# Retention by feature in column tiles, and expert blocks of up to 768 slots whose widths are chosen by branches

## The chip, the cores and the metric

The kernel runs on one core of one Trainium2 chip. Times are microseconds (us) of device time. The core has a matrix engine (TensorE, "PE" in the profile; its weight loads are shown apart as "PEld"), a vector engine (DVE), an activation engine (ACT), GpSimd (POOL) and a sync engine (SP), and 16 DMA engines that move data for all of them. A "record" is one matmul as the profile lists it; each float32 product appears as two (the 8 score products of a chunk as 16). In a PE line, 128*64 is the piece of the array in use, rows by columns, and a column tile is a half of its 128 columns used on its own.

## The reference

```python
# 8 batches, 8 heads, 576 positions, head_dim 64; all float32
scores = q @ k.T / 8
ret = scores * gamma[h] ** (i - j)          # for j <= i, else 0
x = (ret @ v)                               # by token: 4608 tokens x 512
logits = x @ w_gate;  local = sigmoid(x @ w_local)
for each batch, for each position s in order:
    e = argmax(logits[s]) if s == 0 or local[s] < 0.5 else the expert of s-1
    out[s] = softmax(logits[s])[e] * (relu(x[s] @ w1[e]) @ w2[e])   # 512 -> 1024 -> 512, 8 experts
```

On these inputs each expert receives 517 to 652 tokens; the prediction lists all eight counts.

## The kernel before

It has three stages. **Retention** runs over 36 chunks of 128 tokens, with a state per head carried from chunk to chunk. Per chunk it transposes k on PE, makes the scores, the outputs by token, and the new state; then it transposes x on PE and makes the logits from it:

```python
for c in range(HP): nc.tensor.transpose(kps[:, c, :], kn[:, c * P:(c + 1) * P], ident)
...
for h in range(H):          # outputs by token: the scores are stationary, 64 columns of V stream
    nc.tensor.matmul(ops[:, h, :], lhsT=sT[:, h % 2, h // 2, :], rhs=vs[:, h * DH:(h + 1) * DH], ...)
...
for c in range(HP):         # state: k of two heads is stationary (only the diagonal blocks are used)
    nc.tensor.matmul(kv[:, c, :], lhsT=kn[r, c * P:(c + 1) * P], rhs=vs[r, c * P:(c + 1) * P], ...)
...
for c in range(DK): nc.tensor.transpose(xps[:, c, :], x[:, c * P:(c + 1) * P], ident)
for c in range(DK): nc.tensor.matmul(lps[:, i, :], lhsT=xT[:, c, :], rhs=wg[:, c, :], ...)
```

**Routing** finds each token's expert and its slot, and the token of each slot, by a long chain of small operations. **Experts**: the slots of an expert are padded to blocks of 256; there are always 25 blocks, the most that any routing can need. Each block loads its expert's weights, gathers its tokens with indirect DMAs, transposes them and runs both layers:

```python
for j in range(NBLK):                               # 25
    e = nc.values_load(eid[0:1, j:j + 1], engines=[ET.SP], ...)   # only the weight loads depend on it
    ... load w1[e], w2[e] (4.2 MB) ...
    for u in range(SUB): ... gather, 4 transposes, copy ...       # SUB = 2
    for m in range(0, FK, 2): ... hidden layer, 256 columns, relu on ACT ...
    for u in range(SUB):
        ... second product (8 matmuls of 512 columns), scale, scatter ...
```

The language's scheduler lays out the order of instructions on each engine; it may place independent work of a later block ahead.

## Time and profile before

| | us |
|---|---|
| time, median of 4 runs | 1039.3 (1037.8 to 1045.9) |
| retention ends at | 250.3 |
| routing, to the first hidden pass | 44.9 |
| experts | 731.2 |
| tail, after the last product | 11.2 |

These are the busy shares of the page of the kernel before, and two of its rows of 40 equal slices of the span (a digit is tenths busy; PEclk is the clock that PE was granted, in tenths of full speed). PE is the bound nearly everywhere, and the dip in the tenth to twelfth slice is routing.

```profile
PE 974.9 (94%) x4918; PEld 719.0 (69%) x4918; DVE 166.8 (16%) x282; ACT 123.8 (12%) x238; POOL 140.7 (14%) x158
...
PE   7999999996479999999999999999999999999995
...
PEclk9999999998589999999999999999999999999998
```

A busy PE says that it executes something, not that it does so at its best rate. So the useful numbers are starts in the timeline, from one group of records to the next, as the prediction uses them.

### The profile page before, as it was taken

The page shows a single profiled execution, that of the slowest core. Times are in us where ns is not written, and L with a number is a line of the kernel's source. Part 1 is how long each engine was busy: PE and PEld are TensorE (multiplying, and loading weights), DVE is VectorE, ACT ScalarE, POOL GpSimd, SP SyncE. Part 2 cuts the span into 40 slices and gives each one's busy share as a digit, 9 for nine tenths or more (in the row PEclk, how much of TensorE's full clock was granted, in tenths as well). Part 3 has the DMA queues.
Part 4 walks back from the last instruction along what each step waited for, and adds up shares of the span by engine and source line. Part 5 has one row for each costly group of instructions (what it writes and reads, how often), then busy time and mean ns, then how long its engine had stood idle before and what let it go on. Part 6 is the DMA issues. An engine that isn't in the chain of part 4 may idle for free. (4 is left out here: it accounts for less than half of the span.)

```text
span 1037.5 us, 12062 instructions
## 1 busy us (share of the span) xinstructions
PE 974.9 (94%) x4918; PEld 719.0 (69%) x4918; DVE 166.8 (16%) x282; ACT 123.8 (12%) x238; POOL 140.7 (14%) x158
## 2 busy tenths in 40 slices
PE   7999999996479999999999999999999999999995
PEld 6999999995466666666666666666666666666662
DVE  2333332324711111010111111010111110010100
ACT  2222222221000000000000000000000000000000
POOL 2111111110021111011111110011111110110000
PEclk9999999998589999999999999999999999999998
DMA  5444444430735544555455544555455544555300
GB/s 201 154 158 157 151 163 162 163 133 32 273 122 203 201 156 148 185 197 177 153 179 187 193 156 153 181 193 188 138 187 203 164 158 160 195 183 167 127 2 0
DMA packets 47509, 166.03 MB, mean 160 GB/s; under 512 B 7006, under 2 KB 7134, under 8 KB 47456
## 3 DMA queue, kind: packets, MB, share of 16 engines
q1 hardware_dynamic: 39168, 142.62, 40.5%
q0 software_dynamic: 8000, 22.56, 6.3%
q8 instruction: 39, 0.64, 0.2%
q14 instruction: 14, 0.11, 0.0%
q10 hardware_dynamic: 288, 0.09, 0.0%
HBM read 146.37 MB, written 22.54 MB: 163 GB/s over the span
## 5 line engine op out<-in xcount | busy, mean ns | idle before, releaser
L395 PE MATMUL hps<-xTs,w1s 128*128 128x256 f32 x1600 | 353.2, 382 | 14.1 <-DVE xTs L389 14.1
L402 PE MATMUL yps<-w2s,hT 128*128 128x512 f32 x800 | 347.4, 592 | 0.0
L395 PEld LDWEIGHTS hps<-xTs,w1s 128*128 128x128 f32 x1600 | 303.0, 191 | 60.2 <-DVE xTs L389 19.8
L402 PEld LDWEIGHTS yps<-w2s,hT 128*128 128x128 f32 x800 | 152.0, 190 | 180.7 <-issue 179.4
L405 DVE TENSOR_SCALAR y<-yps,pslot 128x512 f32<-128x512 f32 x50 | 37.5, 751 | 665.4 <-PE yps L402 665.4
L397 ACT ACTIVATE hT<-hps 128x512 f32<-128x512 f32 x100 | 59.7, 597 | 700.2 <-PE hps L395 700.2
L406 POOL DMA_INDIRECT out_dram<-y,sidx x50 | 50.7, 1014 | 512.0 <-DVE y L405 505.3
L139 PE MATMUL ops<-vs,sT 128*128 128x64 f32 x576 | 82.3, 277 | 0.0
L139 PEld LDWEIGHTS ops<-vs,sT 128*128 128x128 f32 x576 | 72.4, 191 | 4.9 <-issue 0.6
L127 DVE TENSOR_TENSOR sT<-sps,mask 128x512 f32<-128x512 f32 x72 | 46.4, 686 | 159.9 <-PE sps L123 159.9
L383 POOL DMA_INDIRECT xg<-xd,gidx x50 | 48.7, 975 | 164.0 <-PE xgps L388 121.2
L116 POOL TENSOR_TENSOR vs<-ld,dec 128x512 f32<-128x512 f32 x36 | 37.5, 1042 | 190.0 <-PE kv L155 173.2
L123 PE MATMUL sps<-ld,kT 64*128 64x128 f32 x576 | 43.2, 288 | 0.2 <-DVE sT L127 0.2
L161 ACT COPY state<-kv 64x256 f32<-64x256 f32 x64 | 23.4, 366 | 160.2 <-PE kv L155 159.4
L176 PE MATMUL lps<-wg,xT 128*128 128x9 f32 x288 | 38.0, 259 | 1.5 <-ACT xT L174 1.1
L176 PEld LDWEIGHTS lps<-wg,xT 128*128 128x128 f32 x288 | 34.9, 191 | 5.2 <-ACT xT L174 4.7
L123 PEld LDWEIGHTS sps<-ld,kT 64*128 64x128 f32 x576 | 36.3, 190 | 2.9 <-DVE sT L127 0.4
L388 PEld LDWEIGHTS xgps<-ident,xg 128*128 128x128 f32 x200 | 24.2, 146 | 20.1 <-issue 19.5
L155 PE MATMUL kv<-vs,ld 128*128 128x128 f32 (+1 forms) x256 | 35.5, 281 | 0.5 <-ACT state L161 0.5
L146 PE MATMUL ops<-state,ld 128*128 128x128 f32 (+1 forms) x256 | 35.4, 281 | 0.0
L388 PE MATMUL xgps<-ident,xg 128*128 128x128 f32 x200 | 27.7, 282 | 6.6 <-DMA xg<-xd,gidx 6.6
L389 DVE COPY xTs<-xgps 128x512 f32<-128x512 f32 x50 | 32.2, 682 | 7.1 <-PE xgps L388 7.1
(112 smaller groups left out, 271.2 us busy)
## 6 DMA issues: line engine op xcount, KB each, us to landing
w1s<-in_w_dram SPq DMA_DIRECT2D x100, 512.0 KB, 5.5
w2s<-in_w_dram SPq DMA_DIRECT2D x100, 512.0 KB, 8.1
ld<-in_qkv_dram SPq DMA_DIRECT2D x36, 768.0 KB, 4.5
xd<-x SPq DMA_DIRECT2D x36, 256.0 KB, 2.2
xg<-xd,gidx POOLq DMA_INDIRECT x50, 7.3
out_dram<-y,sidx POOLq DMA_INDIRECT x50, 7.5
dec<-in_decay_dram ACTq DMA_DIRECT2D x1, 72.0 KB, 4.6
wg<-in_wgl_dram ACTq DMA_DIRECT2D x1, 18.0 KB, 6.2
```

The source lines that it names most:

```text
L116: nc.gpsimd.tensor_tensor(vs.rearrange("p (h d) -> p h d", h=H), vn.rearrange("p (h d) -> p h d", h=H), dec[:, 1, m, :].unsqueeze(2).to_br ...
L123: nc.tensor.matmul(sps[u][:, c, :], lhsT=kT[r, c, :], rhs=qT[r, c, :], start=True, stop=True, skip_group_check=True)
L127: nc.vector.tensor_tensor(sT[:, u], sps[u], (mask2 if m == MID else mask).unsqueeze(1).to_broadcast([P, HP, P]), op=Alu.mult)
L139: nc.tensor.matmul(ops[:, h, :], lhsT=sT[:, h % 2, h // 2, :], rhs=vs[:, h * DH:(h + 1) * DH], start=(h == 0), stop=(m == 0), skip_group_c ...
L176: nc.tensor.matmul(lps[:, i, :], lhsT=xT[:, c, :], rhs=wg[:, c, :], start=(c == 0), stop=(c == DK - 1), skip_group_check=True)
L383: nc.gpsimd.indirect_dma_start(out=xg, out_offset=None, in_=xd, in_offset=bass.IndirectOffsetOnAxis(ap=gidx[:, s:s + 1], axis=0))
L388: nc.tensor.transpose(xps[:, c, :], xg[:, c * P:(c + 1) * P], ident)
L395: nc.tensor.matmul(hps[:, v, :], lhsT=w1s[:, m + v, c, :], rhs=xT[:, c, :], start=(c == 0), stop=(c == DK - 1), skip_group_check=True)
L397: nc.scalar.activation(hT[:, m:m + 2, :], hps, Act.Relu)
L402: nc.tensor.matmul(yps, lhsT=hT[:, m, u * P:(u + 1) * P], rhs=w2s[:, m, :], start=(m == 0), stop=(m == FK - 1))
L405: nc.vector.tensor_scalar(y, yps, pslot[:, s:s + 1], None, Alu.mult)
L406: nc.gpsimd.indirect_dma_start(out=out, out_offset=bass.IndirectOffsetOnAxis(ap=sidx[:, s:s + 1], axis=0), in_=y, in_offset=None, bounds_c ...
```

## The change

In retention it wants fewer and cheaper PE records: k is also loaded transposed; outputs are made by feature (V stationary with 64 columns, two heads in two column tiles of the array), kv likewise; x by token and the logits come from one product with the identity and the gates side by side. In the experts it wants less padding: one block holds up to 768 slots of an expert, and branches on the number of tokens held choose the width of two hidden passes and how many product groups run.

```diff
-T = 256  # tokens of one expert that go through its weights together
+T = 768
+PASS = T // 2
 NBLK = (NTOK - E) // T + E
+ALWAYS = -(-NTOK // T)
+WIDTHS = (128, 192, 224, 256, 288, 320, 352, PASS)
... (retention)
-            for c in range(HP):
-                nc.tensor.transpose(kps[:, c, :], kn[:, c * P:(c + 1) * P], ident)
+            kT = ld[:, 1].rearrange("p (c s) -> p c s", c=HP)
...
+                for c in range(HP):
+                    for u in range(2):
+                        h = 2 * c + u
+                        nc.tensor.matmul(kv[half(u), c, :], lhsT=kn[r, h * DH:(h + 1) * DH],
+                                         rhs=vs[r, h * DH:(h + 1) * DH], ...)
...
+            for c in range(HP):
+                for u in range(2):
+                    h = 2 * c + u
+                    nc.tensor.matmul(ops[half(u), c, :], lhsT=vs[:, h * DH:(h + 1) * DH],
+                                     rhs=sT[:, u, c, :], ...)
...
+            for c in range(DK):
+                nc.tensor.matmul(nps[:, c, 0:P + E + 1], lhsT=xT[:, c, :], rhs=gates[:, c, :], ...)
... (experts)
+    def by_width(held, base, widths, body):
+        if len(widths) == 1:
+            body(widths[0])
+            return
+        h = len(widths) // 2
+        with tc.If(held > base + widths[h - 1]) as wider:
+            by_width(held, base, widths[h:], body)
+        with wider.Else():
+            by_width(held, base, widths[:h], body)
...
+        by_width(held, 0, WIDTHS, lambda n: hidden(w1s, xT, hT, 0, n))
+        with tc.If(held > PASS):
+            by_width(held, PASS, WIDTHS, lambda n: hidden(w1s, xT, hT, PASS, n))
         for u in range(SUB):
...
+            if u == 0:
+                product()
+            else:
+                with tc.If(held > u * P):
+                    product()
+    for j in range(ALWAYS):          # 6
+        block(j)
+    total = nc.values_load(plan[0:1, 2 * NBLK:], ...)
+    with ExitStack() as rest:
+        for j in range(ALWAYS, NBLK):        # 6 to 12, each inside the branch of the one before
+            rest.enter_context(tc.If(total > j))
+            block(j)
```

## The prediction

> **What bounds the kernel now.** I first read the share of the span by engine: TensorE (PE) 94% busy, no other engine above 16%. Its instructions in order of time show three stages, so I asked for the busy time of each engine in each (columns: stretch; its length; busy us and count of PE, PE weight load, DVE, ACT, POOL; granted clock; DMA share; GB/s).
>
> ```profile
> 5.34:250.30 244.96, 241.58 (x2240) 227.90 (x2240) 71.01 (x108) 62.38 (x136) 37.83 (x38) 1.00 0.45 151
> 250.30:295.17 44.87, 16.23 (x91) 14.27 (x91) 28.52 (x74) 0.44 (x1) 8.24 (x18) 0.58 0.58 212
> 295.17:1027.00 731.83, 717.08 (x2589) 476.79 (x2588) 66.19 (x98) 59.70 (x100) 92.62 (x94) 1.00 0.48 162
> 1027.00:1037.50 10.50, 0.00 (x0) 0.00 (x0) 0.13 (x1) 0.00 (x0) 0.98 (x1) 0.72 0.00 0
> ```
>
> Retention (245 us) and the experts (732 us) are PE-bound, at 98.6% and 98.0% busy. Routing (45 us) is a serial chain, mostly on DVE, at a clock of 0.58. The chain of waits that ended last covers only the final 30 us here, so I price PE work from starts in the timeline: from the start of one group to that of the next, in one retention chunk (start, duration, instruction, count):
>
> ```profile
> 228.26 0.60 PE L172 MATMUL xps<-ident,x 128*128 128x128 f32 x4
> 228.70 0.60 PE L112 MATMUL kps<-ident,ld 128*128 128x128 f32 x4
> 229.13 0.78 PE L139 MATMUL ops<-vs,sT 128*128 128x64 f32 x6
> 229.93 1.06 PE L176 MATMUL lps<-wg,xT 128*128 128x9 f32 x8
> 230.85 0.86 PE L139 MATMUL ops<-vs,sT 128*128 128x64 f32 x6
> 231.64 1.16 PE L123 MATMUL sps<-ld,kT 64*128 64x128 f32 x16
> 232.73 0.66 PE L139 MATMUL ops<-vs,sT 128*128 128x64 f32 x4
> 233.23 1.11 PE L146 MATMUL ops<-state,ld 128*128 128x128 f32 x8
> 234.17 1.06 PE L155 MATMUL kv<-vs,ld 128*128 128x128 f32 x8
> 235.07 0.60 PE L172 MATMUL xps<-ident,x 128*128 128x128 f32 x4
> ```
>
> The period is 235.07 - 228.26 = 6.81 us (36 of them: 245). Each f32 product is two records (8 heads give 16). Per chunk: x transposes 0.44, k transposes 0.43, outputs 0.80+0.79+0.50 = 2.09 (131 ns a record although only 64 columns stream), logits 0.92 (115 ns for 9 columns), scores 1.09 (68 ns), state product 0.94, kv 0.90. Records of 9, 64 and 128 columns cost about the same: with 128 weight columns the weight load paces them. Only the scores, which use 64 rows each, go twice as fast.
>
> One expert block of 256 slots, read in the same way:
>
> ```profile
> 353.27 1.04 PE L388 MATMUL xgps<-ident,xg 128*128 128x128 f32 x8
> 354.88 14.08 PE L395 MATMUL hps<-xTs,w1s 128*128 128x256 f32 x64 [0.57 <-DVE xTs L389]
> 368.80 13.90 PE L402 MATMUL yps<-w2s,hT 128*128 128x512 f32 x32
> 382.53 1.04 PE L388 MATMUL xgps<-ident,xg 128*128 128x128 f32 x8
> ```
>
> Hidden layer: 13.92 us / (64 x 256) = 0.850 ns a column. Second product: 13.73 us for two groups of 128 slots, 6.87 us each. Transposes: 0.52 us a group. Period 29.26; 25 of them are 732. Cost follows slots, padding included: 6400 slots are computed for 4608 tokens.
>
> [...]
>
> **The change, part by part.**
>
> Retention. k arrives transposed too, so 0.43 goes. Outputs are made by feature: 64 columns of V stationary, 128 columns of scores streaming, two heads in two column tiles. Taking the scores' 68 ns for them: 16 x 68 = 1.09 instead of 2.09. kv becomes 16 records with 64 weight columns instead of 8 with 128: at 62 ns (half of a 128-column load plus little) 1.00 instead of 0.90. x and logits: 8 records of 137 columns, 137 x 0.85 = 117 to 120 ns, 0.96, instead of 0.44 + 0.92. Scores 1.09 and state 0.94 stay. Two more mode changes per chunk: 0.15 (a guess: the scores' 68 ns, with their two changes in it, are near the 54 ns that half of 128 columns would take). Sum 5.23 us. DVE (2.06 plus a small reduction), ACT (1.8 less one 0.59 copy) and POOL (1.04) stay below that. DMA moves 1.31 MB per chunk, at 5.2 us 250 GB/s; before, 159 GB/s used half of the engines, and the first 10 us show 314, so 80%: close but hidden. 36 x 5.23 = 188. The start is later: the first load grows from 0.79 to 1.05 MB and shares the engines with a new 1.3 MB decay table (first product at 7.5 instead of 5.3), and two memsets of 6144 elements on POOL (0.8 ns an element from the 288-element one at 0.33 us: 5 us each) may hold back V's scaling. I take 5 us for filling. Retention ends at 201 instead of 250.
>
> Routing. 78 slot groups instead of 50, so the three column operations grow from 2.03 to about 3.17 us (+3.4). The block plan adds some eight small operations at 0.16 to 0.35 us and removes four at 0.17: +1.3. Slot products at half clock, 156 columns instead of 100: +1.5. The first block gathers six groups instead of two, and POOL issues one per 1.25 us: +5. So 45 becomes 56.
>
> Experts. Running the reference's routing on its inputs gives 652, 576, 581, 554, 591, 517, 606 and 531 tokens. All fit one block of 768: eight blocks. Every first pass is 384 wide; the second is 288 once, 224 three times, 192 four times: 4800 columns. Product groups: 6 + 7 x 5 = 41. Transposes: 8 x 6 = 48 groups, unconditional.
> - Hidden: 4800 x 64 x 0.850 ns = 261 (before 25 x 13.92 = 348).
> - Second product: 41 x 6.87 = 282 (before 343).
> - Transposes: 48 x 0.52 = 25 (before 26).
> Sum 568, against 717 of work before. Weights fall from 25 x 4.2 MB to 8 x 4.2 MB; DMA was half idle already, so this buys nothing.
>
> Costs of control flow, which the profile of before can't price:
> - At each block PE waits for ACT's last hidden group (one 0.6 us evacuation plus the hand-over) and DVE's last copy (0.57 above): 1.3. Branches: some 10 compares, and two or three jumps over 500 to 900 PE instructions[...]. [...] 8 x 3.5 = 28.
> - Blocks 6 and 7 stand inside branches, so I expect their gathers can't be placed ahead of the branch: on POOL they follow block 5's last scatter, which waits for the product. Then PE stands still for DVE's 0.75, the scatter's 1.0, a register load, six gathers at 1.25, about 2.4 to land, a transpose and a copy: some 15 us, less 3 of work counted above, plus 1 for the lower clock: 2 x 13 = 26. For blocks 0 to 5 I expect the 12 gather buffers, two blocks' worth, to keep this hidden.
>
> Tail 11.5 (10.5 plus a jump over five blocks). Sum: 201 + 56 + 568 + 28 + 26 + 11.5 = 890 us.
>
> **Rivals.** (a) Column tiles don't overlap: outputs stay at about 115 ns a record, the chunk at 6.0 us, +27: 917. For it: the trace shows only row tiles. [...] (b) Branches dominate: [...]: 990. Against it: PE's queue runs ahead through three PSUM buffers, 7 us of work in a 384-wide pass. (c) Gathers aren't placed ahead in any block: five more stalls of 13 us, 955. In its favour, POOL now waits most of its time for DVE's y in program order; the profile of before shows a scatter, then gathers, interleaved by hand of the scheduler. (d) DMA bounds retention: 1.31 MB at 314 GB/s is 4.2 us, below 5.2, so only the start suffers. (e) Branches nearly free and blocks 6 and 7 prefetched: 890 - 22 - 26 = 842.
>
> **Range and chances.** PE work removed is well measured: about 56 us in retention and 149 in the experts. Some 90 us are given back, two thirds of it estimated. Low end: (e), 842. High end: (c) or half of (b), 965. To lose all 149 us of gain needs more than 18 us per block beyond what I count; I give slower 2% and within 2% 2%.
>
> **What would show it.** A chunk period near 5.2 us with 16-record output groups starting about 1.1 us apart; if (a), 1.8. Eight expert periods of about 65 to 80 us, hidden records at 0.85 ns a column. PE idle before the first transposes of blocks 6 and 7, released by the gather, over 8 us, and hardly any for blocks 1 to 5. PE gaps of 1 to 4 us between the two hidden passes with no releaser in the profile. I am wrong if PE's idle time in the experts is much over 55 us, or if the period in retention follows the loads.

The sum came to 890 us: 201 + 56 + 568 + 28 + 26 + 11.5. Of the 28 us (8 blocks at 3.5) the text above accounts for 1.3 us a block; the other 2.2, for branches, were my own estimate with no trace behind it. So was the 1 us in the tail for the jump over five blocks, and the 1 us for a lower clock in each of blocks 6 and 7, for which the trace of before has only routing to go by (0.50 granted in each of the three windows of 10 us from 250 to 280 us). Rival (b), a cost at each of the roughly 100 branches: no trace stood behind its 990 either. That PE's queue keeps it busy past a branch was an expectation, which the changed kernel bears out below. That the weight load paces the records of retention is my reading of equal times: records of 9, 64 and 128 columns took 115, 131 and 113 to 118 ns, with PEld busy for 227.9 of the 245.0 us. Two more things are in that trace: tiles of 64 rows go at 68 ns a record against 115 to 131, and the queue that carries instructions moved 39 packets, 0.64 MB, so 16 KB each. It has no column tiles.

## The result, and the profile after

The changed kernel takes 879.5 us (median of 4 runs, 878.9 to 880.5) against 1039.3: ratio 0.846, with a 95% interval of 0.843 to 0.849. The prediction said 890, with a range of 842 to 965.

The page of the changed kernel, the same rows as before. PE is less busy as a share, and the later slices have dips in both rows that the kernel before did not have.

```profile
PE 773.6 (88%) x4158; PEld 507.6 (58%) x4158; DVE 171.4 (20%) x312; ACT 100.0 (11%) x230; POOL 138.7 (16%) x155
...
PE   7999999915799999999999799899979599959892
...
PEclk9999999967699999999999899999989899979997
```

The stages, in the columns of the prediction's first view:

```profile
5.90:178.90 173.00, 171.55 (x2208) 151.86 (x2208) 77.96 (x143) 43.91 (x99) 47.80 (x39) 1.00 0.78 273
178.90:229.41 50.51, 17.79 (x94) 15.01 (x95) 32.68 (x82) 1.03 (x2) 9.07 (x22) 0.64 0.55 202
229.41:860.20 630.79, 584.25 (x1856) 340.71 (x1856) 59.08 (x85) 53.78 (x128) 78.61 (x81) 0.96 0.22 74
860.20:877.10 16.90, 0.04 (x1) 0.00 (x0) 0.75 (x1) 0.00 (x0) 0.98 (x1) 0.65 0.03 8
```

Retention fell from 250.3 to 178.9 us and is still PE-bound (171.6 of 173.0 us busy), though its DMA share rose from 0.45 to 0.78. Routing grew by 5.6 us. The experts fell from 731.2 to 630.8, but PE now stands still for 630.8 - 584.3 = 46.5 us of them, and the clock is 0.96 instead of 1.00. The tail grew from 11.2 to 16.9.

One chunk of retention after (start, duration, instruction, count):

```profile
19.29 1.16 PE L130 MATMUL sps<-ld 64*128 64x128 f32 x16
20.38 1.16 PE L149 MATMUL ops<-ld,state 128*128 128x128 f32 x8
21.47 0.69 PE L159 MATMUL kv<-vs,ld 128*64 128x64 f32 x16
21.98 1.05 PE L168 MATMUL ops<-sT,vs 128*64 128x128 f32 x16
22.96 1.21 PE L180 MATMUL nps<-gates,xT 128*128 128x137 f32 x8
24.09 1.16 PE L130 MATMUL sps<-ld 64*128 64x128 f32 x16
```

From start to start: scores 1.09, state product 1.09, kv 0.51, outputs 0.98, x and logits 1.13: a period of 4.80 us where the prediction had 5.23. An output record takes 61 ns and a kv record 32 ns in the mean of its group.

In the experts the idle time has two large parts. The first stands before or in second hidden passes (19.2 of the 21.5 us before hidden passes), and the profile names no releaser ("issue"). Here is one in the timeline, after the last product group of a block and ten records of the next block's first group:

```profile
454.30 27.69 PE L449 MATMUL yps<-w2s,hT 128*128 128x512 f32 x64
482.29 4.53 PE L449 MATMUL yps<-w2s,hT 128*128 128x512 f32 x10 [0.30 <-PEq L460]
492.13 12.80 PE L399 MATMUL hps<-xTs,w1s 128*128 128x192 f32 x64 [5.32 <-issue]
504.77 2.74 PE L449 MATMUL yps<-w2s,hT 128*128 128x512 f32 x6
```

The branches are on record too, as instructions of PE's sequencer. These are those of the width tree (line 409): over the whole run, then between 482 and 493 us alone, with shortest, median and longest in ns.

```profile
L409 PEldq COMPARE_BRANCH  x64: 65/136/6899, 228.5 to 826.3; - x64
```

```profile
L409 PEldq COMPARE_BRANCH  x3: 70/3616/5816, 482.5 to 492.0; - x3
```

So two of the three branches ahead of that pass took 5.82 and 3.62 us. Together they last from 482.5 to 492.0, while the ten queued product records kept PE going only until 486.8: the difference is the 5.3 us gap. The pass after it takes 504.77 - 492.13 = 12.64 us where a pass of this width takes 10.4 at full clock (341.98 to 352.38 in the same trace), because PE's clock had dropped in the gap: the trace grants 0.50 from 489.7 to 496.5. Of the 64 such branches 22 took over 3 us (3.2 to 3.8 us in 16 of them, 4.7 to 6.9 in six), and within each of the 22 the trace has a fetch of 16 KB of instructions of 0.9 to 2.2 us (two fetches in two of them). The others took 0.34 us at most. On ACT and POOL the branches of this line had a median of 38 ns, on DVE 47. The queue that carries instructions doubled its packets, first before, then after:

```profile
q8 instruction: 39, 0.64, 0.2%
```

```profile
q8 instruction: 78, 1.28, 0.6%
```

The second part of the idle time is in blocks 6 and 7, those inside the branches on the number of blocks. PE's timeline at block 6, and POOL's beside it:

```profile
661.35 29.35 PE L449 MATMUL yps<-w2s,hT 128*128 128x512 f32 x68
700.12 4.82 PE L437 MATMUL xgps<-ident,xg 128*128 128x128 f32 x20 [9.42 <-DMA xg<-xd,gidx]
705.28 0.63 PE L437 MATMUL xgps<-ident,xg 128*128 128x128 f32 x4 [0.35 <-DMA xg<-xd,gidx]
706.20 20.88 PE L399 MATMUL hps<-xTs,w1s 128*128 128x384 f32 x64 [0.29 <-issue]
```

```profile
691.76 0.98 POOL L453 DMA_INDIRECT out_dram<-y,sidx  x1 [5.88 <-DVEq L460]
694.56 0.99 POOL L432 DMA_INDIRECT xg<-xd,gidx  x1 [1.81 <-issue]
695.86 0.98 POOL L432 DMA_INDIRECT xg<-xd,gidx  x1 [0.30 <-issue]
```

The last product ended at 690.7; POOL issued block 5's last scatter at 691.8 and only then block 6's first gather, and PE waited 9.4 us for it. The next hidden pass began 15.5 us after the product's end.

### The profile page after: what moved, and what is told of

It is laid out like the page before. It is cut to its first block, busy times and chain, and to the rows that moved or that the text cites. A ratio compares the mean times of both kernels' runs of the same rounds, so it can differ in the third digit from the quotient of the medians. Undisturbed runs are those within 1.5% of the kernel's fastest.

```text
span 877.1 us, 10692 instructions
## 1 busy us (share of the span) xinstructions
PE 773.6 (88%) x4158; PEld 507.6 (58%) x4158; DVE 171.4 (20%) x312; ACT 100.0 (11%) x230; POOL 138.7 (16%) x155
## 4 chain that ended last, share of the span: by engine, by line
issue 33%; DMA 12%; PE 5%; POOL 1%; POOLq 0%; DVE 0%; another core or an unknown queue 0%
DMA out_dram<-y,sidx 11%; PE hps L399 4%; PE yps L449 1%; POOL xg L432 1%; PE xgps L437 0%; DMA xg<-xd,gidx 0%; POOLq L460 0%; POOL out_dram L453 0%; POOLq L453 0%; DVE xTs L438 0%; DVE y L452 0%; POOLq L417 0%; POOLq L432 0%; POOLq L467 0%
## 5 line engine op out<-in xcount | busy, mean ns | idle before, releaser
L399 PE MATMUL hps<-xTs,w1s 128*128 128x384 f32 (+3 forms) x1024 | 272.7, 429 | 21.5 <-issue 21.5
L449 PE MATMUL yps<-w2s,hT 128*128 128x512 f32 x656 | 285.1, 593 | 0.6 <-PEq L460 0.6
L399 PEld LDWEIGHTS hps<-xTs,w1s 128*128 128x128 f32 x1024 | 194.6, 198 | 100.9 <-issue 32.4
L401 ACT ACTIVATE hT<-hps 128x384 f32<-128x384 f32 (+3 forms) x128 | 53.8, 420 | 594.5 <-PE hps L399 594.5
L124 POOL TENSOR_TENSOR vs<-ld,deck 128x512 f32<-128x512 f32 x36 | 37.5, 1043 | 115.4 <-DMA ld<-in_qkv_dram 59.0
L130 PE MATMUL sps<-ld 64*128 64x128 f32 x576 | 44.9, 296 | 6.4 <-DMA ld<-in_qkv_dram 6.4
L130 PEld LDWEIGHTS sps<-ld 64*128 64x128 f32 x576 | 37.8, 198 | 11.4 <-DMA ld<-in_qkv_dram 6.7
L180 PE MATMUL nps<-gates,xT 128*128 128x137 f32 x288 | 43.4, 292 | 0.9 <-DVE lt L184 0.9
L168 PE MATMUL ops<-sT,vs 128*64 128x128 f32 x576 | 38.9, 278 | 0.0
L149 PE MATMUL ops<-ld,state 128*128 128x128 f32 (+1 forms) x256 | 36.7, 286 | 0.0
```

What stands on the lines that cost most here:

```text
L124: nc.gpsimd.tensor_tensor(vs.rearrange("p (h d) -> p h d", h=H), vn.rearrange("p (h d) -> p h d", h=H), deck[:, m, :].unsqueeze(2).to_broa ...
L130: nc.tensor.matmul(sps[u][:, c, :], lhsT=kT[half(u), c, :], rhs=qT[half(u), c, :], start=True, stop=True, skip_group_check=True)
L149: nc.tensor.matmul(ops[:, c, 0:n], lhsT=states[(i + 1) % 2][:, c, :], rhs=qT[:, c, 0:n], start=(c == 0), stop=False, skip_group_check=True)
L168: nc.tensor.matmul(ops[half(u), c, :], lhsT=vs[:, h * DH:(h + 1) * DH], rhs=sT[:, u, c, :], start=(m == 0 and c == 0), stop=True, skip_gro ...
L180: nc.tensor.matmul(nps[:, c, 0:P + E + 1], lhsT=xT[:, c, :], rhs=gates[:, c, :], start=True, stop=True, skip_group_check=True)
L399: nc.tensor.matmul(hps[:, 0:n], lhsT=w1s[:, m, c, :], rhs=xT[:, c, base:base + n], start=(c == 0), stop=(c == DK - 1))
```

## The experiments

All ten kernels give the right result. In each table of this section "experts" is the stretch from the first hidden pass to PE's last product, and "idle" is that stretch less PE's busy time in it.

| run | time, us | experts | idle | clock in experts |
|---|---|---|---|---|
| the changed kernel | 879.5 | 630.8 | 46.5 | 0.96 |
| eight_always | 853.5 | 604.2 | 28.0 | 0.98 |
| first_pass_fixed | 861.3 | 606.5 | 32.5 | 0.98 |
| narrow_first | 859.0 | 608.5 | 32.2 | 0.98 |
| four_widths | 846.0 | 597.8 | 22.8 | 0.98 |
| one_width | 918.9 | 668.7 | 24.5 | 0.98 |
| combined | 825.2 | 575.1 | 8.1 | 1.00 |
| no_branches (this input only) | 807.2 | 568.8 | 5.4 | 1.00 |

### Are the two halves independent?

The first run puts the new retention stage into the kernel before; the second puts the new routing and experts behind the old retention.

```diff
 # retention_only: before, with the retention stage, the decay tables and the input layout of the changed kernel
 # experts_only: the changed kernel, with those of before
```

> The new retention stage with routing and experts as before. If the two halves of the change are independent: retention ended at 250.3 us in the kernel before and ends at 178.9 in the changed one, 71 us less, so about 968 us and a chunk period of 4.80. If part of the retention gain came with the new experts (lighter weight traffic beside it, an earlier start), the period is nearer 5.2 us and the time 980.

> The old retention stage with the new routing and experts. Independent halves: the whole change saved 160 us, less the 71 of retention leaves 89, so about 950 us. If the halves help each other, this one saves under 75 us (965 or more).

They took 966.5 us (966.2 to 966.9; ratio to before 0.929) and 955.2 us (952.7 to 957.0; ratio 0.918). Against the 1039.6 of the same rounds they save 73.1 and 84.4 us, together 157.5; the whole change saves 159.8. The halves add up to within 2.3 us, which is inside the spread of the second run. Retention alone also has the period of 4.80 us, so nothing of its gain comes from the lighter weight traffic.

### Do column tiles overlap?

Rival (a) of the prediction said that they might not. The edit keeps every product and only changes the order, so that neighbours share a tile:

```diff
-            for c in range(HP):
-                for u in range(2):
+            for u in range(2):
+                for c in range(HP):
                     h = 2 * c + u
                     nc.tensor.matmul(ops[half(u), c, :], ...)      # and likewise for kv
```

> The same output and kv products, but the four of one column tile first and then the four of the other, so that neighbours share a tile. Theory: outputs at 61 ns a record and kv at 32 ns come from two tiles working side by side; in one tile an output record costs its 128 columns, 109 ns, and a kv record 57 ns or so: period from 4.80 to about 6.0 us, 920 us in all. Rival: a weight load of 64 columns is what makes them fast: no change, 879.

It took 899.2 us (898.4 to 899.8), 19.7 more than the changed kernel. One chunk that ends a pair of sequences, and so has no kv:

```profile
101.79 1.16 PE L149 MATMUL ops<-ld,state 128*128 128x128 f32 x8
102.88 1.58 PE L168 MATMUL ops<-sT,vs 128*64 128x128 f32 x16
104.39 1.21 PE L180 MATMUL nps<-gates,xT 128*128 128x137 f32 x8
```

The outputs take 104.39 - 102.88 = 1.51 us instead of 0.98, 94 ns a record instead of 61. In the other chunks kv and outputs together take 2.08 us (106.62 to 108.70 in this trace) instead of 1.49. Alternating between the two tiles is therefore what gives this part of the gain, and the rival (the smaller weight load alone) falls. But the loss was half of what I expected: I had priced a record in a single tile at 0.85 ns for each of 128 columns, 109 ns, and the mean came to 94. The starts of the single records in this chunk of the trace show why. Within a tile they are 109 ns apart, as priced; but where the order goes over from the first tile to the second, five steps in a row are 53 to 57 ns, so there the two tiles still overlap. The smaller tile by itself therefore gains next to nothing: the old output records start 112 ns apart within a group, and the 131 ns of the prediction is a mean that contains the breaks between their three groups.

### What keeps the gathers of blocks 6 and 7 late?

```diff
-ALWAYS = -(-NTOK // T)
+ALWAYS = 8
```

> All eight blocks that this input needs stand outside the conditional region (the other five stay in it). Theory: only the branch around blocks 6 and 7 keeps their gathers from being placed ahead; the stretch from the last product to the next hidden pass was 15.5 us in both, of which about 3 us is transpose work, and block 7's first pass ran 2.2 us slow at a lower clock. So about 27 us less: 852 us, and PE waits for a gather only in block 0. Rival: POOL's place behind the scatters is set by the buffers and not by the branch: 877 to 880.

It took 853.5 us (851.5 to 857.0), ratio to before 0.822: 26 us less than the changed kernel. What PE waited for, over the whole run; first the changed kernel, then this one (total us, times, longest):

```profile
PE xgps L437 <- DMA xg<-xd,gidx: 25.0, 8, 9.4
PE hps L399 <- issue: 21.5, 11, 5.3
```

```profile
PE hps L399 <- issue: 20.0, 11, 5.6
...
PE xgps L437 <- DMA xg<-xd,gidx: 7.2, 4, 6.2
```

The waits for gathers fell to those of block 0, and the waits called "issue" stayed. The experts lost 26.6 us. The branch around a block did it: the scheduler placed no gather from inside it ahead of it, although buffers for two blocks are there.

### What do the branches cost in all?

The edit in short (the loads of the counts and the blocks beyond the eighth go too):

```diff
+        # eight blocks, everything from this input's counts, no tc.If anywhere; NBLK = 8
+        hidden(w1s, xT, hT, 0, PASS)
+        hidden(w1s, xT, hT, PASS, (288, 192, 224, 192, 224, 192, 224, 192)[j])
         for u in range(SUB):
+            if u < 5 or j == 0:
+                product()
```

> Eight blocks with the pass widths and product counts of this input written in: no branch at all (right for this input only). Theory: of PE's 95 us in branches that wait for instructions, only what isn't covered by queued matmuls counts, the 21 us that PE stood still before hidden passes, plus some 5 us of lower clock after it and 6 us in the tail: about 820 us, 32 below the run with eight blocks outside. Rival 1: the branches are covered anyway, so only the tail: 846. Rival 2: they also hinder the placing of other work: under 810.

It took 807.2 us (806.6 to 807.5). The experts of this kernel, and of the one with eight blocks outside:

```profile
225.46:794.30 568.84, 563.41 (x1854) 329.43 (x1852) 58.69 (x85) 53.89 (x128) 78.28 (x81) 1.00 0.23 81
```

```profile
229.50:833.70 604.20, 576.21 (x1856) 336.37 (x1856) 58.51 (x85) 53.79 (x128) 78.61 (x81) 0.98 0.23 78
```

The same arithmetic takes 35.4 us less: 28.0 - 5.4 = 22.6 us less idle time, and 576.2 - 563.4 = 12.8 us less busy time. Most of that is the clock (1.00 instead of 0.98): weighing PE's busy time in the experts with the clock granted at each moment, 7.9 us are lost to half clock with eight blocks outside, and none here. I had allowed 5. The other 4.9 us of busy time I can't assign. The total of 807.2 is under the 810 at which I would have said that branches also hinder the placing of other work. This run doesn't decide that, because part of the excess is a side effect of the edit: 8 blocks have 48 slot groups instead of 78, the routing tables are smaller, and the first hidden pass began 46.2 us after retention instead of 50.4. The tail is 10.2 us. The expert stretch is the clean comparison.

### Is the choice of width worth its branches?

```diff
-WIDTHS = (128, 192, 224, 256, 288, 320, 352, PASS)
+WIDTHS = (PASS,)
```

> Only 384-wide passes: no choice of width, but the branch for the second pass stays. 6144 columns instead of 4800 add 1344 x 64 x 0.843 ns = 72 us. Theory: the width branches cost about 25 us at the end (21 of PE idle, the rest clock), which comes back: about 925 to 930. Rival: their fetches are hidden: 950.

It took 918.9 us (915.0 to 920.3). The experts grew by 37.9 us instead of the 72 that the columns alone cost, so the eight-way tree was costing about 35 us: again idle time (46.5 to 24.5) and clock (7.8 us, weighed as above), 10 us more than the expectation had. The choice still pays, by 39 us.

### Does a fetch cost time wherever it stands?

Three runs ask this. The first removes the tree of the first pass, which on this input always ends in the same width; its jumps over the other seven bodies took 3.2 to 3.7 us each.

```diff
-        by_width(held, 0, WIDTHS, lambda n: hidden(w1s, xT, hT, 0, n))
+        hidden(w1s, xT, hT, 0, PASS)
```

> The first pass is always 384 wide (as it is on this input anyway): its three compares and its jump over the seven narrower bodies go. Each of these jumps took 3.2 to 3.7 us on PE's sequencer. Theory: they start while two or three groups of 2.6 us are queued, so PE doesn't notice: 876 to 880. Rival: each jump costs its time: 8 x 3.5 = 28 us, 851.

It took 861.3 us (854.8 to 861.8 in 6 runs; the profile is of one of 856.3), 18 us less: my theory's number missed. In the trace of the changed kernel none of the idle time follows a first pass, so these jumps were indeed covered. What the edit changed is the order. This is a second pass in the new kernel:

```profile
460.82 20.16 PE L399 MATMUL hps<-xTs,w1s 128*128 128x384 f32 x62
480.82 1.02 PE L449 MATMUL yps<-w2s,hT 128*128 128x512 f32 x2
483.01 10.88 PE L399 MATMUL hps<-xTs,w1s 128*128 128x192 f32 x64 [1.17 <-issue]
```

With the first pass outside a branch, the scheduler put most of it directly ahead of the second pass. The two jumps (3.43 us from 476.2, 3.12 from 479.7) now run under its last groups, and 1.2 us show. Also, the longest branches are gone: the longest here is 3.84 us, while four in the changed kernel took 5.8 to 6.9. In those four the fetch began 3.4 to 4.5 us after the branch instead of about 1. The traces show what stood beside them. Over the first 2 us after each of the four, the queue that carries the weights kept the 16 DMA engines 58% to 97% busy: SP had begun to issue four loads of w2 0.4 to 1.9 us before. In the nine kernels with such branches, 140 of PE's branches took over 2 us; in 19 of them the fetch began more than 2 us after the branch, and all 19 had 58% or more of such traffic, against 11 of the other 121 with over 30%. No run moved the loads, so that they are the cause is likely and not shown.

The second turns the tree of the second pass over, so that narrow bodies come first and the long jump comes after the body (the part that changes; `by_width` is called with it for the second pass only):

```diff
+            with tc.If(held < base + widths[h - 1] + 1) as low:
+                by_width(held, base, widths[:h], body, True)
+            with low.Else():
+                by_width(held, base, widths[h:], body, True)
```

> The tree of widths of the second pass turned over, narrow bodies first: for 192 and 224 columns PE falls into or near the body and jumps after it, with the pass queued, instead of jumping twice before it. Theory: a fetch costs time only where nothing is queued behind it: most of the 21 us of idle before second passes goes, and 4 us of low clock: 855 to 862. Rival: number of fetches counts wherever they stand: within 5 us of 879.

It took 859.0 us (858.7 to 865.6), as expected. The same pass as shown above, 192 columns after ten records of a first product group:

```profile
484.45 4.53 PE L455 MATMUL yps<-w2s,hT 128*128 128x512 f32 x10 [0.30 <-PEq L466]
488.82 10.56 PE L399 MATMUL hps<-xTs,w1s 128*128 128x192 f32 x64
499.65 2.84 PE L455 MATMUL yps<-w2s,hT 128*128 128x512 f32 x6 [0.27 <-issue]
```

The same ten records are queued, and no gap follows. The jump with its fetch, 3.28 us, now starts at 496.3, while the pass still has 3 us to run, and costs 0.3 us. The kernel fetched nearly as often (73 packets against 78). So it is not the number of fetches that counts but what PE has queued when one begins. Part of the 20 us may be something else: the turned tree also has no late fetch (its longest branch takes 4.25 us), and no run separates the two. A late fetch is not needed for a gap, though: in the changed kernel two jumps from 810.1 to 818.4, with no weights moving, left PE idle for 3.20 us, while the two from 334.4 to 341.2 ran under the end of a group of 90 product records and left none.

The third shortens the distances:

```diff
-WIDTHS = (128, 192, 224, 256, 288, 320, 352, PASS)
+WIDTHS = (192, 224, 288, PASS)
```

> Four widths (192, 224, 288, 384) instead of eight: this input's passes keep their widths, the tree has two levels, and the jumps ahead of a second pass of 192 or 224 columns skip 256 and at most 128 PE instructions instead of 512 and 128 to 256. Theory[...]: one fetch before a second pass instead of two, idle before hidden passes from 21 to about 8 us, 860 to 866. Rival: the count of compares matters, not the distance: 3 fewer per block at 0.1 us, 877.

The distances in the trace of the changed kernel are these. All seven jumps over 512 PE instructions ahead of second passes waited for a fetch, and so did the four over 256 that followed for 192 columns; of the three over 128 that followed for 224 columns one did.

It took 846.0 us (845.7 to 846.7), below the expectation. Waits for "issue" before hidden passes fell from 21.5 to 0.3 us in total (I had left 8), and PE's busy time in the experts fell by 9.3 us, 6.7 of them by the better clock, which I had not counted. The packets fell to 61.

### A version that keeps the choices and beats both

```diff
+ALWAYS = 8
+WIDTHS = (192, 224, 288, PASS)
+        hidden(w1s, xT, hT, 0, PASS)               # the first pass without a tree
+            by_width(held, PASS, WIDTHS, ..., narrow=True)
+            if u < 5:                              # the first five product groups outside branches
+                product()
```

> What the runs so far point to, all choices still made from the data: eight blocks outside the conditional region, first pass always 384 wide, second pass of four widths with the narrow bodies first, the first five product groups of a block outside branches. No branch at all gave 807 us; the five conditional blocks cost 6.6 us in the tail, the one jump after each second pass is covered by it. If the theory holds: 814 to 822, and idle PE before hidden passes under 4 us. If branches also cost through the order of work: 830 or more.

It took 825.2 us (822.4 to 829.5 in 6 runs), ratio to before 0.794 (0.790 to 0.797), 54 us below the changed kernel; the median is a little above the expected 814 to 822. Its experts:

```profile
230.75:805.80 575.05, 567.00 (x1853) 330.12 (x1852) 58.39 (x84) 53.67 (x128) 78.08 (x80) 1.00 0.23 80
```

That is 6.2 us above the kernel without any branch. The rest of the 18 us between the two spans is 5.3 us of an earlier first hidden pass there (mostly the smaller tables, as I read it) and 6.4 us of tail. By its construction it is right for any routing, but all runs here used one input. And it is tuned to balanced routings: an expert with few tokens would pay for a full first pass and five product groups, and a routing with fewer than eight blocks for empty ones.

## Why the prediction was right, point by point

The total was 890 against 879.5, and the mechanism held in both halves; the sum was closer than its parts.

- **Retention (predicted to end at 201, ended at 178.9).** The mis-sized terms were the period, 5.23 against 4.80 us, the start, and chunks that are shorter than the period. Outputs were right (1.09 predicted, 0.98 measured; rival (a) falls). kv was sized at 1.00 us, with half of a 128-column weight load per record; it took 0.51, because there too the two tiles work side by side: the two records of a pair start 6 to 7 ns apart in the chunk above, and with one tile at a time the first 13 kv records of a chunk took 0.57 us, 44 ns each instead of 32. I had applied this to the outputs and not to kv. The state product and the x product came out 0.15 and 0.17 longer than sized, 0.32 together where I had guessed 0.15 for the mode changes. The starts of single records in the chunk above show where it goes. At each of its four changes of shape (scores, state product, kv and outputs, x and logits) the step to the first record of the new shape is 202 to 208 ns, and the next one (for the two-tile groups, the next pair) is longer too: 213 and 221 where 112 and 116 to 120 follow. From kv to outputs, where the shape stays, the step is 51. The period less the steady steps leaves about 0.18 us a change (an estimate from these starts), so two more of them are 0.36, not 0.15; no run removed a change. From the first product to the end retention took 173.0 us, which happens to be 36 times 4.81. But 36 full periods are more than the work: of the nine chunks of a pair the first has no state product and the last no kv, which saves 4 x (1.09 + 0.51) = 6.4 us. The start loses 4.9 of them again: its groups run slower, the first two of scores 2.08 and 2.67 us instead of 1.16. So the 5 us for filling were about right, and what the sum left out was the short chunks; that the two nearly cancel is chance. The first product came at 5.9 us, not 7.5. The memsets on POOL (5.22 us each, as estimated) held nothing up that PE waited for. The loads did not set the period (rival (d)).
- **Routing (56 predicted, 50.5 measured).** The column operations grew by 3.1 us in all (3.4 worked out). The gathers added 1.9 instead of 5, since the first pass of 384 slots started after four of the six groups were transposed. The larger slot products cost 0.3 instead of 1.5.
- **Expert work (568 predicted).** The kernel without branches has 568.8 us from the first hidden pass to the last product, its idle 5.4 included. This count of columns and groups is the best part of the prediction.
- **Blocks 6 and 7 (26 predicted).** Taking them out of the branches gave 26.6 us in the experts. The mechanism was as described, and rival (c), late gathers in all blocks, falls: in blocks 1 to 5 PE waits for no gather.
- **Waits and branches (28 predicted).** The difference between eight_always and no_branches is 35.4 us. The step was right that some taken branches wait for fetches (22 of the 64 width branches) and that queued matmuls cover part of it (none of PE's idle time followed the jumps after first passes, 3.2 to 3.7 us each). Its parts were off: I had 10 us for ACT's last group and DVE's last copy, but PE never waited for ACT before a product there, because the first product group, which needs only the first pass, stands outside the branches. The larger omission is the clock: about 8 us of the 35.4 are PE running at half clock after gaps. I had counted a lower clock only for blocks 6 and 7. In the trace of the changed kernel gaps of 3.27, 4.66 and 5.32 us went with 3.4 to 6.8 us at 0.50, one of 3.20 with none.
- **Tail (11.5 predicted, 16.9 measured).** I took the old tail as 10.5, but it was 11.2, and gave the skipped blocks 1 us. The kernel without them has 10.2. PE's branch over them took 3.4 us by itself.
- **What would show me wrong.** I had named an idle time "much over 55 us" in the experts; it was 46.5. Rival (b), a cost at each of the branches, falls: 42 of the 64 width branches took under 0.4 us, and narrow_first has nearly the same number of fetches at 20 us less.

Retention came out 22 us and routing 5.5 us better than predicted, control flow (28 and 26) with the expert work 9 us and the tail 5.4 us worse; these sum to the 13 us by which the span (877.1) lies under 890. That the total came so close owes something to luck: the errors are 28 us one way and 14 the other.

## What to carry to other kernels

Price a data-dependent branch by what its engine has queued when it jumps: put the likely body first and the long jump behind it (narrow_first: 859.0 us against 879.5), keep untaken bodies few (four_widths: 846.0), and hoist what nearly always runs out of the branch, so that the scheduler can order it and gathers can be placed ahead (eight_always: 853.5). Look also at what the DMA engines carry at that moment: the fetches that came late here all met weight loads (19 of 19). Count the clock as well as the gap: here about a fifth of what the branches cost (7.9 of 35.4 us) was PE at half clock after standing still. Small products gained from column tiles here only where neighbours lay in different tiles: output records start 112 ns apart with 128 weight columns, 109 within one tile, and 55 in the mean when they alternate. So order them so. And count the changes of tile shape, about 0.18 us each here.
